# One user per score tile at the end, a shared block of last keys, and a later landing for bulk loads in the planned order

## The chip, the cores and the metric

The kernel runs on one core of a Trainium2 chip, as one program with one launch. The metric is the device time of that program in microseconds; four runs are at hand, and one more execution was profiled. The engines are PE (matrix products; PEld is its loading of weights), DVE, ACT and POOL (elementwise work), and SP, which here only issues DMAs.

## What is computed

Eight batches of eight heads, 576 rows of 64 numbers each. The attention keeps only scores within `tau` = 0.02 of their row's largest, and its output is laid side by side for the eight heads to give 4608 tokens of 512 numbers, which go through a normalised gated feed-forward layer:

```python
scores = scale * np.matmul(q, k.transpose(0, 1, 3, 2))
thresh = np.max(scores, axis=-1, keepdims=True) - tau
scores = np.where(scores >= thresh, scores, -1000000000.0)
scores = scores - np.max(scores, axis=-1, keepdims=True)
attn = np.exp(scores)
attn = attn / (np.sum(attn, axis=-1, keepdims=True) + 1e-09)
x = np.matmul(attn, v)                  # then heads side by side: (4608, 512)
rms = np.sqrt(np.mean(x * x, axis=-1, keepdims=True) + 1e-06)
xn = x / rms * rms_g
g = xn @ w_gate
silu = g * (1.0 / (1.0 + np.exp(-g)))
val = xn @ w_val
out = (silu * val @ w_out)              # (512, 1536), (512, 1536), (1536, 512)
```

## The kernel before

**Tiling.** Every 128 rows of queries make a chunk: four from the first 512 rows of each batch ("m"), and one from the last 64 rows of two batches together ("v"). That gives 36 chunks, and with four pairs of heads each 144 steps. The 576 keys of a head are four blocks of 128 and a last one of 64. For the even head of a pair the probabilities lie as main blocks and then last keys, for the odd head as last keys and then main blocks, so that in the row of 1152 probabilities block 4 of nine holds the last 64 keys of both heads, one above the other.

**A step.** `emit_s` makes the scores on PE (fp32, L566) into the two score tiles `s_ps0` and `s_ps1`, one for each head. Each is 1024 columns of PSUM, two banks; a head's 576 scores lie across the boundary. DVE reads them (`ttr`, L589) and takes the row maxima; POOL makes the threshold (`nth`, L596); ACT, and POOL for some heads, make the probabilities `wsb` in fp16 (L607, L611, L614, L626, L640, L645). They are transposed into `wt`, by PE in the first 16 steps (L659) and by a DMA on SP's queue after that (L674).

**Product with the values.** After every second step `emit_av` multiplies two pairs of heads (L696). For each head it runs five products of 65 columns (64 values and a column of ones that gives the row sum). For the block of last keys it uses entry 8 of `va` for the even head, whose lower 64 rows are zero, and entry 9 for the odd head, whose upper 64 rows are zero. All four heads share one PSUM slot. DVE divides by the row sums (L712, L713) and `emit_x` normalises (L724 to L732) and transposes by DMA (L736).

**Feed-forward.** `emit_ffn` takes groups of two or four chunks (`SIZES`), so products of 256 or 512 columns. For each of twelve blocks of the hidden layer there is a gate product (`gmm`, L790) and a value product (`vmm`, L795), a tanh on ACT (L804), and two steps on DVE: `silu` (L807) and `gate` (L812), whose result is the fp16 block `hf`. The output products follow when all twelve blocks are there, six at a time (L849). Only the last group, of two chunks, is "streamed": its output products (L829) are interleaved with the gate and value products, `OUT_LAG` blocks behind, and two PSUM slots accumulate through the whole group. The result is moved to `osb` by ACT (L863), or for the second chunk of the streamed group by DVE (L861), and stored by SP (L868).

**PSUM slots.** Gate, value and output products, products with the values and transposes share a ring of four slots of one bank, tiles of their own. After the last score step the four banks of the two score tiles become four more slots, 4 and 5 in `s_ps0`, 6 and 7 in `s_ps1` (`opens`, set at L952). PSUM slots are assigned by the plan; waits between instructions are placed by the tile framework from the tiles that they touch.

**The order.** Every piece of work is an `Op` with an engine, an estimated cost, a priority and the pieces that it needs. `order_ops` plays the engines forward in time: it takes, over all engines, the piece that can start first, ties by priority, and writes out that order. Each engine runs its queue in it. A DMA's end is planned from one shared DMA stream (`dma_free`, which advances by the transfer's own `DMA_NS`) plus a latency: `LAT_TR` = 3000 ns for a transposing DMA and 2000 ns for any other. Loads of queries, keys, values and weights that are marked `bulk` may not start more than `BACKLOG` ahead of that stream. At the start the first keys come by ACT's queue (bulk), the first queries and last keys by SP's (`load_q0`, `load_kt`, not bulk).

Of the kernel before, what the change touches and what calls it, by code (L numbers as in the profile page):

```python
# [13 lines left out]
SEM = 160.0  # L14
SLACK = 0.0
COST = dict(
    s_main=932.0, s_virt=900.0, tr_qk=530.0, tr4=230.0, tr_full=440.0, av_main=320.0, av_virt=500.0, ffn4=216.0, warm=3500.0,
    ttr=690.0, evac_qk=600.0, evac_half=380.0, evac_kt=350.0, prelu=700.0, exp2=1250.0, exp1=690.0, exp0=690.0,
    mask_d=750.0, mask_g=1740.0, take_g=1300.0, trw=510.0, evac_w=450.0, evac_wp=900.0, rz=180.0, xmul=420.0, sq=800.0, xn=720.0,
    pool_tiny=270.0, pool_mean=800.0, pool_dma=850.0, cast_v=650.0, cast_vt=420.0, cast_w=720.0,  # L20
# [4 lines left out]


class Op:
    __slots__ = ("eng", "cost", "prio", "deps", "fn", "ring", "frees", "slot", "end", "start", "dma", "opens", "nring", "mode", "bulk", "release")

    def __init__(self, eng, cost, prio, deps, fn, ring=None, frees=None, dma=0.0, nring=1, mode=0, bulk=False):  # L30
        self.eng, self.cost, self.prio, self.fn = eng, cost, prio, fn
        self.deps = [d for d in deps if d is not None]
        self.ring, self.frees, self.dma = ring, frees, dma
        self.slot = self.end = self.start = None
        self.opens = ()
        self.nring = nring
        self.mode = mode
        self.bulk = bulk
        self.release = 0.0


def order_ops(ops, ring_sizes):


    import heapq

    ring_free = {r: [(0.0, i) for i in range(n)] for r, n in ring_sizes.items()}
    users = {}
    left = {}
    for i, o in enumerate(ops):  # L50
        left[i] = len(o.deps)
        for d in o.deps:
            users.setdefault(id(d), []).append(i)
    pending = {}
    for i, o in enumerate(ops):
        pending.setdefault(o.eng, [])
        if not left[i]:
            pending[o.eng].append(i)
    eng_free = {e: 700.0 for e in pending}
    dma_free = 0.0  # L60
    mode = 0
    out = []
    ready_at = {i: 0.0 for i in range(len(ops))}
    while len(out) < len(ops):
        best = None
        for e, lst in pending.items():
            if not lst:
                continue
            t0 = eng_free[e]
            cand = None  # L70
            for i in lst:
                o = ops[i]
                t = max(t0, ready_at[i])
                if o.ring is not None:
                    if len(ring_free[o.ring]) < o.nring:
                        continue
                    t = max(t, sorted(ring_free[o.ring])[o.nring - 1][0])
                other = e == "PE" and o.mode != mode
                t = max(t, o.release)
                if o.bulk:  # L80
                    t = max(t, dma_free - BACKLOG)
                k = (t + (BIAS if other else 0.0), o.prio, i)
                if cand is None or k < cand:
                    cand = k
            if cand is not None and (best is None or cand < best[0]):
                best = (cand, e)
        (t, _, i), e = best
        o = ops[i]
        cost = o.cost
        if e == "PE":  # L90
            if o.mode != mode:
                t -= BIAS
                cost += SWITCH
            mode = o.mode
        o.start = t
        if o.ring is not None:
            o.slot = []
            for _ in range(o.nring):
                got = min(ring_free[o.ring])
                ring_free[o.ring].remove(got)  # L100
                o.slot.append(got[1])
        eng_free[e] = t + cost
        if o.dma:
            dma_free = max(dma_free, t + 300.0) + o.dma
            o.end = max(dma_free, t + o.cost) + (LAT_TR if o.cost == COST["sp_tr"] else 2000.0)
        else:
            o.end = t + cost
        if o.frees is not None:
            ring_free["R"].append((o.end + SEM, o.frees[0].slot[o.frees[1]]))
        for slot in o.opens:  # L110
            ring_free["R"].append((o.end + SEM, slot))
        pending[e].remove(i)
        out.append(o)
        for j in users.get(id(o), []):
            u = ops[j]
            wait = 0.0 if u.eng == o.eng and not o.dma else SEM + (SLACK if u.eng == "PE" else 0.0)
            ready_at[j] = max(ready_at[j], o.end + wait)
            left[j] -= 1
            if not left[j]:
                pending[u.eng].append(j)  # L120
    return out
# [3 lines left out]
def kernel(  # L125
# [12 lines left out]
    nc = tc.nc  # L138
    B, H, S, D = q.shape
# [78 lines left out]
    def add(eng, cost, prio, deps, fn, **kw):  # L218
        o = Op(eng, cost, prio, deps, fn, **kw)
        ops.append(o)  # L220
        return o
# [455 lines left out]
            w_read[s] = t  # L677
            w_ready[s] = [t]

    V_AT = ((0, 2, 4, 6, 8), (9, 1, 3, 5, 7))  # L680

    def emit_av(s):

        ci, p1 = steps[s]
        kind, b, c = chunks[ci]
        hp = p1 // 2

        def fn(o):
            for i in range(2):
                w, p = wt[(s - 1 + i) % NWT], p1 - 1 + i  # L690
                for h in range(2):
                    at = (2 * i + h) * (D + 1)
                    rows = [(slice(0, 128), b % 2)] if kind == "m" else [(HALF[e], e) for e in range(2)]
                    for rs, vi in rows:
                        for j in range(5):
                            nc.tensor.matmul(ring[o.slot[0]][rs, at:at + D + 1], w[:, 4 * h + j, rs],  # L696
                                             va[vi][:, p, V_AT[h][j]], start=(j == 0), stop=(j == 4))

        bs = [b] if kind == "m" else [2 * b, 2 * b + 1]
        deps = w_ready[s - 1] + w_ready[s] + [x for bb in bs for i in range(2) for x in v_ready[bb, p1 - i]]  # L700
        o = add("PE", 2 * COST["av_main" if kind == "m" else "av_virt"], s + AV_PRIO, deps, fn, ring="R",
                mode=0 if kind == "m" else 3)
        for i in range(2):
            av_of[s - i] = [o]
            for bb in bs:
                last_av[bb, p1 - i] = last_av.get((bb, p1 - i), []) + [o]

        r = rz[len(half_ev) % 3]

        def half(_):  # L710
            o3 = ring[o.slot[0]][:, 0:4 * (D + 1)].rearrange("p (h d) -> p h d", d=D + 1)
            nc.vector.reciprocal(out=r, in_=o3[:, :, D])  # L712
            nc.vector.tensor_tensor(  # L713
                out=xsb[ci % 2][:, 256 * hp:256 * hp + 256].rearrange("p (h d) -> p h d", d=D),
                in0=o3[:, :, 0:D], in1=r[:, :, None].to_broadcast([128, 4, D]), op=ALU.mult)

        half_ev.append(add("DVE", COST["rz"] + COST["xmul"], s + HALF_PRIO, [o] + x_done.get(ci - 2, []), half,
                           frees=(o, 0)))
# [48 lines left out]
    def emit_ffn(slot, parts, ready_step, pace, streamed):  # L767
# [55 lines left out]
        if streamed:  # L823

            acc = None
            for fc, (hi, m_) in enumerate(hs):
                def omm(o, fc=fc, hi=hi, first=acc):
                    for j in range(len(parts)):
                        nc.tensor.matmul(ring[(first or o).slot[j]], hf[hi][:, 128 * j:128 * (j + 1)], wo[:, fc],  # L829
                                         start=(fc == 0), stop=(fc == NFC - 1))  # L830

                mo = add("PE", len(parts) * COST["ffn4"], st + dt * (fc + OUT_LAG), [m_] + wo_ld + outs[-1:], omm,
                         ring=None if acc else "R", nring=len(parts))
                acc = acc or mo
                outs.append(mo)
                hf_use[hi] = [mo]
        for j, (ci, _) in enumerate(parts):
# [24 lines left out]
                else:  # L862
                    nc.scalar.activation(out=osb[oi], in_=ring[mo.slot[at]], func=AF.Copy, scale=0.5)  # L863

            def store(o, oi=oi, kind=kind, b=b, c=c):
                if kind == "m":
                    dst = out[b * S:b * S + MAIN].rearrange("(si sc) d -> si sc d", sc=4)[:, c]
                    nc.sync.dma_start(out=dst, in_=osb[oi])  # L868
                else:
                    for e in range(2):  # L870
                        r0 = (2 * b + e) * S + MAIN
# [1 line left out]

            e = add("DVE" if late else "ACT", 690.0 if late else 620.0, pr - PUSH[0], [outs[-1], osb_use.get(oi)], ev,
                    frees=(mo, at))
            osb_use[oi] = add("SP", COST["sp"] if kind == "m" else 1100.0, pr, [e], store, dma=DMA_NS['out'])
        if not streamed:
            for hi, _ in hs:
                hf_use[hi] = list(outs)
# [69 lines left out]
        if step > 0:  # L949
            o.deps.append(s_of[int(step)])  # L950
    for h in range(2):
        ttr_of[len(steps) - 1, h].opens = (4 + 2 * h, 5 + 2 * h)  # L952
    seq = order_ops(ops, {"R": 4})
    global LAST_SEQ
    LAST_SEQ = seq
# [3 lines left out]


PACE = 13.0
NHF = 16
SIZES = (2, 2, 2, 2, 4, 4, 4, 4, 4, 4, 2, 2)
LAG = 16.0
LAT_TR = 3000.0
REL = (0.0, 0.0)
REL_N = (0, 0)
STREAMED = 1
OUT_LAG = 3.0
OUT_PART = 6  # L970
ELAG = 16.0
NELAG = 0
# [58 lines left out]
```

## Time and profile before

| What | Value |
|---|---|
| Median of four runs | 574.64 us (574.57 to 575.74) |
| Profiled execution | 574.66 us, of it the span of the program's instructions 572.9 us |
| Granted TensorE clock | 1.00 |
| DVE, scores to `ssb` (L589) | 288 instructions, mean 753 ns |
| ACT, probabilities (L607) | 224 instructions, mean 766 ns |
| PE, output products in blocks of six (L849), 512 columns | 384 instructions, 89.3 us busy |
| Loads to landing, median | values 3.1 us, keys 3.3, queries 3.2, gate weights 4.2, value weights 4.7 |
| Stores to landing, median | 2.7 us |
| Transposing DMAs of probabilities | 128, 3.1 us to landing |

Times in the views are microseconds from the start of the span unless marked as ns. A line of the timeline gives start, length, engine, line, operation, the tile written and the tiles read, shapes, and how many instructions were merged; in brackets the engine's idle time ahead and what ended it. A line of the chain of waits gives start, length and what was waited for. Matmuls are pipelined and their ends are modelled, so the distance from one start to the next says more of PE than a length.

### The profile page before, as it was taken

How to read it: one execution, taken by the hardware profiler on the slowest of the kernel's cores; microseconds unless marked ns; L12 is line 12 of the kernel's file. 1: busy time of each engine (PE TensorE's matmuls, PEld its weight loads, DVE VectorE, ACT ScalarE, POOL GpSimd, SP SyncE). 2: the span in 40 equal slices, each digit the busy share in tenths (PEclk: the TensorE clock that was granted, in tenths of full speed). 3: DMA queues.
4: the chain of work that ended last, by engine and by line, in shares of the span. 5: the costliest groups of instructions: out<-in, count | busy, mean ns of one | idle time of the engine just before them, and what ended most of it. 6: DMA issues, size and time to landing. Idle time of an engine off the chain costs nothing.

```text
span 572.9 us, 14110 instructions
## 1 busy us (share of the span) xinstructions
PE 560.3 (98%) x5160; PEld 333.9 (58%) x5160; DVE 426.4 (74%) x1093; ACT 459.6 (80%) x739; POOL 322.5 (56%) x462
## 2 busy tenths in 40 slices
PE   8989999999999999999999999999999999999995
PEld 4666776767767555555555455555555455554763
DVE  4898986868958688659974889578867886585543
ACT  3998998998979788879988997888978997883322
POOL 1367856876657456665765667565666665541000
PEclk9999999999999999999999999999999999999999
DMA  7899999768995679968977597867788454641111
GB/s 173 224 268 253 235 178 214 140 134 191 176 195 121 129 156 168 168 172 183 155 181 169 118 167 175 193 165 147 165 193 171 104 105 112 142 93 48 56 38 37
DMA packets 271173, 89.01 MB, mean 155 GB/s; under 512 B 253696, under 2 KB 263424, under 8 KB 271104
## 3 DMA queue, kind: packets, MB, share of 16 engines
q1 hardware_dynamic: 268448, 86.28, 69.4%
q0 software_dynamic: 1600, 1.57, 1.8%
q8 instruction: 40, 0.66, 0.5%
q10 hardware_dynamic: 1056, 0.26, 0.2%
q14 instruction: 29, 0.24, 0.2%
HBM read 37.75 MB, written 9.44 MB: 82 GB/s over the span
## 4 chain that ended last, share of the span: by engine, by line
PE 88%; POOL 3%; DMA 3%; ACT 2%; DVE 2%; issue 2%; SPq 0%; ACTq 0%; DVEq 0%; POOLq 0%
PE s_ps L566 28%; PE ring L795 15%; PE ring L790 15%; PE ring L849 14%; PE ring L696 7%; PE ring L302 2%; DMA vst<-in_v_dram 1%; PE s_ps L790 1%; PE s_ps L795 1%; PE ring L364 1%; PE s_ps L829 1%; PE s_ps L849 1%; ACT ssb L607 1%; DVE ssb L589 1%; DMA qkn<-in_k_dram 1%
## 5 line engine op out<-in xcount | busy, mean ns | idle before, releaser
L589 DVE CUSTOM_DVE_ANT_0 ssb<-s_ps,zrow 128x576 f32<-128x576 f32 x288 | 206.8, 753 | 61.8 <-PE s_ps L566 52.9
L607 ACT ACTIVATE ssb<-ssb,nth 128x576 f32<-128x576 f32 x224 | 165.6, 766 | 26.7 <-POOL nth L596 26.2
L566 PE MATMUL s_ps<-qkt 64*128 64x288 f32 x1024 | 172.3, 432 | 1.4 <-DVE mx L589 1.1
L566 PEld LDWEIGHTS s_ps<-qkt 64*128 64x128 f32 x1024 | 96.4, 187 | 55.7 <-DVE mx L589 14.0
L640 POOL TENSOR_SCALAR wsb<-ssb,nth 128x576 f16<-128x576 f32 x64 | 110.5, 1726 | 11.5 <-ACT ssb L607 3.9
L790 PE MATMUL ring<-xnT,wg 128*128 128x512 f16 (+1 forms) x524 | 108.4, 329 | 0.1
L795 PE MATMUL ring<-xnT,wv 128*128 128x512 f16 (+1 forms) x520 | 107.5, 329 | 0.3 <-DVE xsb L713 0.3
L596 POOL TENSOR_SCALAR nth<-mx 128x2 f32<-128x2 f32 x144 | 31.6, 220 | 133.0 <-DVE mx L589 123.3
L614 ACT ACTIVATE wsb<-ssb 128x1152 f16<-128x1152 f32 x80 | 93.0, 1163 | 2.3
L849 PE MATMUL ring<-wo,hf 128*128 128x512 f16 x384 | 89.3, 380 | 0.0
L804 ACT ACTIVATE th<-ring 128x512 f32<-128x512 f32 (+1 forms) x131 | 63.6, 487 | 29.6 <-PE ring L790 24.1
L645 POOL TENSOR_TENSOR wsb<-wsb,esb 128x576 f16<-128x576 f16 x64 | 81.8, 1278 | 9.7 <-ACT esb L626 4.9
L807 DVE SCALAR_TENSOR_TENSOR sl<-th,ring 128x512 f32<-128x512 f32 (+1 forms) x131 | 72.9, 556 | 15.9 <-ACT th L804 15.5
L812 DVE TENSOR_TENSOR hf<-ring,sl 128x512 f16<-128x512 f32 (+1 forms) x130 | 73.0, 562 | 12.6 <-PE ring L795 4.1
L795 PEld LDWEIGHTS <-wv 128*128 128x128 f16 x576 | 51.7, 98 | 43.9 <-issue 14.5
L790 PEld LDWEIGHTS <-wg 128*128 128x128 f16 x576 | 52.1, 98 | 40.7 <-issue 10.6
L849 PEld LDWEIGHTS <-hf 128*128 128x128 f16 x408 | 37.4, 98 | 47.0 <-issue 6.6
L696 PEld LDWEIGHTS <-wt 128*128 128x128 f16 (+1 forms) x1600 | 51.5, 100 | 18.5 <-issue 9.8
L696 PE MATMUL ring<-va,wt 128*128 128x65 f16 (+1 forms) x1580 | 56.3, 194 | 0.1
L626 ACT ACTIVATE esb<-ssb,nth 128x576 f16<-128x576 f32 x64 | 49.2, 769 | 5.1 <-POOL nth L596 4.9
L611 ACT ACTIVATE wsb<-ssb 128x576 f16<-128x576 f32 x64 | 43.6, 682 | 1.7
L713 DVE TENSOR_TENSOR xsb<-ring,rz 128x256 f32<-128x256 f32 x71 | 30.1, 424 | 2.5
(65 smaller groups left out, 419.9 us busy)
## 6 DMA issues: line engine op xcount, KB each, us to landing
vst<-in_v_dram SPq DMA_DIRECT2D x32, 256.0 KB, 3.1
out_dram<-osb SPq DMA_DIRECT2D x32, 256.0 KB, 2.7
qkn<-in_k_dram SPq DMA_DIRECT2D x62, 128.0 KB, 3.3
qkn<-in_q_dram SPq DMA_DIRECT2D x56, 128.0 KB, 3.2
stage<-in_moe_w_gate_dram SPq DMA_DIRECT2D x12, 256.0 KB, 4.2
stage<-in_moe_w_val_dram SPq DMA_DIRECT2D x12, 256.0 KB, 4.7
wt<-wsb SPq DMA_TRANSPOSE x128, 3.1
wo<-in_moe_w_out_dram POOLq DMA_DIRECT2D x4, 384.0 KB, 6.5
```

The lines of the kernel that those rows point to most:

```text
L566: nc.tensor.matmul(s_ps[h][rows, ROW_AT + n * part:ROW_AT + n * part + n], lhs(hs), kT[i][p][h][hs, n * part:n * part + n], start=True, st ...
L589: nc.vector.tensor_tensor_reduce(out=ssb[a][:, h], in0=s_ps[h][:, ROW_AT:ROW_AT + S], in1=zrow, scale=-1.0 / 8.0, scalar=3.0e38, op0=ALU.a ...
L607: nc.scalar.activation(out=ssb[a][:, h], in_=ssb[a][:, h], func=PRELU, scale=-1.0, bias=nth[m][:, h:h + 1], **PRELU_KW)
L614: nc.scalar.activation(out=wsb[s % NW], in_=ssb[a], func=AF.Exp)
L640: nc.gpsimd.tensor_scalar(out=wsb[s % NW][:, h], in0=ssb[a][:, h], scalar1=nth[m][:, h:h + 1], scalar2=None, op0=ALU.is_le)
L645: nc.gpsimd.tensor_tensor(out=wsb[s % NW][:, h], in0=wsb[s % NW][:, h], in1=esb[es], op=ALU.mult)
L696: nc.tensor.matmul(ring[o.slot[0]][rs, at:at + D + 1], w[:, 4 * h + j, rs], va[vi][:, p, V_AT[h][j]], start=(j == 0), stop=(j == 4))
L790: nc.tensor.matmul(ring[o.slot[0]][:, 0:n], wg[d][:, fs], xnT[slot][:, d, 0:n], start=(d == 0), stop=(d == 3))
L795: nc.tensor.matmul(ring[o.slot[0]][:, 0:n], wv[d][:, fs], xnT[slot][:, d, 0:n], start=(d == 0), stop=(d == 3))
L807: nc.vector.scalar_tensor_tensor(out=sl[i][:, 0:n], in0=th[i][:, 0:n], scalar=1.0, in1=ring[g.slot[0]][:, 0:n], op0=ALU.add, op1=ALU.mult)
L812: nc.vector.tensor_tensor(out=hf[hi][:, 0:n], in0=ring[vv.slot[0]][:, 0:n], in1=sl[i][:, 0:n], op=ALU.mult)
L849: nc.tensor.matmul(ring[(first or o).slot[0]], hf[hs[fc][0]][:, 128 * j:128 * (j + 1)], wo[:, fc], start=(fc == 0), stop=(fc == NFC - 1))
```

## The change

The product with the values takes the block of last keys once for both heads of a pair: one product of 130 columns against entries 8 and 9 of `va` together opens the accumulation, and then each head adds its four main blocks. So a pair has nine products for ten; the planned costs of the two forms are lowered.

At the end only one slot in each score tile is opened, slot 4 in `s_ps0` and slot 6 in `s_ps1`. An `Op` can now name the slots that it may take (`pick`), and the streamed group's accumulators may take only 4 and 6. `OUT_LAG` goes from 3 to 5. The store of the second chunk of the streamed group is issued by ACT in place of SP.

In the plan a bulk load now ends `LAT_LD` = 3000 ns behind its transfer, where it was 2000.

```diff
-    s_main=932.0, s_virt=900.0, tr_qk=530.0, tr4=230.0, tr_full=440.0, av_main=320.0, av_virt=500.0, ffn4=216.0, warm=3500.0,
+    s_main=932.0, s_virt=900.0, tr_qk=530.0, tr4=230.0, tr_full=440.0, av_main=310.0, av_virt=480.0, ffn4=216.0, warm=3500.0,
...
+        self.pick = None
...
                 if o.ring is not None:
-                    if len(ring_free[o.ring]) < o.nring:
+                    free = [f for f in ring_free[o.ring] if o.pick is None or f[1] in o.pick]
+                    if len(free) < o.nring:
                         continue
-                    t = max(t, sorted(ring_free[o.ring])[o.nring - 1][0])
+                    t = max(t, sorted(free)[o.nring - 1][0])
...
-                got = min(ring_free[o.ring])
+                got = min(f for f in ring_free[o.ring] if o.pick is None or f[1] in o.pick)
...
-            o.end = max(dma_free, t + o.cost) + (LAT_TR if o.cost == COST["sp_tr"] else 2000.0)
+            o.end = max(dma_free, t + o.cost) + (LAT_TR if o.cost == COST["sp_tr"] else LAT_LD if o.bulk else 2000.0)
...
-    V_AT = ((0, 2, 4, 6, 8), (9, 1, 3, 5, 7))
...
-                for h in range(2):
-                    at = (2 * i + h) * (D + 1)
-                    rows = [(slice(0, 128), b % 2)] if kind == "m" else [(HALF[e], e) for e in range(2)]
-                    for rs, vi in rows:
-                        for j in range(5):
-                            nc.tensor.matmul(ring[o.slot[0]][rs, at:at + D + 1], w[:, 4 * h + j, rs],
-                                             va[vi][:, p, V_AT[h][j]], start=(j == 0), stop=(j == 4))
+                rows = [(slice(0, 128), b % 2)] if kind == "m" else [(HALF[e], e) for e in range(2)]
+                for rs, vi in rows:
+
+                    at = 2 * i * (D + 1)
+                    nc.tensor.matmul(ring[o.slot[0]][rs, at:at + 2 * (D + 1)], w[:, 4, rs],
+                                     va[vi][:, p, 8:10].rearrange("p e d -> p (e d)"), start=True, stop=False)
+                    for h in range(2):
+                        for j in range(4):
+                            nc.tensor.matmul(ring[o.slot[0]][rs, at:at + D + 1], w[:, 5 * h + j, rs],
+                                             va[vi][:, p, 2 * j + h], start=False, stop=(h == 1 and j == 3))
+                        at += D + 1
...
-                acc = acc or mo
+                if not acc:
+
+                    acc, mo.pick = mo, ACC
...
-                    nc.sync.dma_start(out=dst, in_=osb[oi])
+                    (nc.scalar if late else nc.sync).dma_start(out=dst, in_=osb[oi])
...
-            osb_use[oi] = add("SP", COST["sp"] if kind == "m" else 1100.0, pr, [e], store, dma=DMA_NS['out'])
+            late = late and kind == "m"
+            osb_use[oi] = add("ACT" if late else "SP", COST["sp"] if kind == "m" else 1100.0, pr, [e], store,
+                              dma=DMA_NS['out'])
...
-        ttr_of[len(steps) - 1, h].opens = (4 + 2 * h, 5 + 2 * h)
+        ttr_of[len(steps) - 1, h].opens = OPENS[h]
...
+ACC = (4, 6)
+OPENS = ((4,), (6,))
+LAT_LD = 3000.0
-OUT_LAG = 3.0
+OUT_LAG = 5.0
```

More of the change, by code (lines that the diff above doesn't have):

```diff
@@ L27 @@
 class Op:
-    __slots__ = ("eng", "cost", "prio", "deps", "fn", "ring", "frees", "slot", "end", "start", "dma", "opens", "nring", "mode", "bulk", "release")
+    __slots__ = ("eng", "cost", "prio", "deps", "fn", "ring", "frees", "slot", "end", "start", "dma", "opens", "nring", "mode", "bulk", "release", "pick")
     def __init__(self, eng, cost, prio, deps, fn, ring=None, frees=None, dma=0.0, nring=1, mode=0, bulk=False):
@@ L863, in ev, with store @@
                     nc.scalar.activation(out=osb[oi], in_=ring[mo.slot[at]], func=AF.Copy, scale=0.5)
-            def store(o, oi=oi, kind=kind, b=b, c=c):
+            def store(o, oi=oi, kind=kind, b=b, c=c, late=late):
                 if kind == "m":
                     dst = out[b * S:b * S + MAIN].rearrange("(si sc) d -> si sc d", sc=4)[:, c]
-                    nc.sync.dma_start(out=dst, in_=osb[oi])
+                    (nc.scalar if late else nc.sync).dma_start(out=dst, in_=osb[oi])
                 else:
```

## The prediction

> **What bounds the kernel now.** I read the page's engine line first, then the chain of waits, then the timeline of single stretches: the steady middle, the last 25 us, the first 9 us.
>
> ```profile
> PE 560.3 (98%) x5160; PEld 333.9 (58%) x5160; DVE 426.4 (74%) x1093; ACT 459.6 (80%) x739; POOL 322.5 (56%) x462
> L566 PE MATMUL s_ps<-qkt 64*128 64x288 f32 x1024 | 172.3, 432 | 1.4 <-DVE mx L589 1.1
> L696 PE MATMUL ring<-va,wt 128*128 128x65 f16 (+1 forms) x1580 | 56.3, 194 | 0.1
> ```
>
> PE is the bound, but 98% busy does not say dense: busy time is modelled and overlaps. The start-to-start times say where PE is dense. From the chain of waits (start, length, what, count):
>
> ```profile
> 19.89 1.91 PE s_ps L566 x8
> 22.52 0.50 PE ring L659 x9
> 44.77 6.77 DMA vst<-in_v_dram
> 226.83 1.17 PE s_ps L566 x8
> 512.54 0.61 PE ring L696 x20
> ```
>
> A step's eight score matmuls take 1.17 us all through the middle. 128 such groups would be 149.8 us; they are busy 172.3, so 22.5 us are lost inside them, nearly all in the first 180 us, where lengths of 1.2 to 1.9 us are common and the chain leaves PE (between 30 and 60 us it runs over POOL, SP and DMA). From 180 to 510 us the chain is PE and nothing else: there only fewer PE nanoseconds help. The end shows PE waiting in a pattern (PE rows with ACT and DVE beside them; in brackets the idle time and its releaser):
>
> ```profile
> 549.80 0.60 PE L790 MATMUL s_ps<-xnT,wg 128*128 128x256 f16 x4
> 550.65 0.60 PE L795 MATMUL s_ps<-xnT,wv 128*128 128x256 f16 x4 [0.25 <-ACT osb L863]
> ...
> 552.83 0.60 PE L790 MATMUL s_ps<-xnT,wg 128*128 128x256 f16 x4
> 553.26 0.59 PE L829 MATMUL s_ps<-wo,hf 128*128 128x512 f16 x2
> 553.70 0.60 PE L795 MATMUL s_ps<-xnT,wv 128*128 128x256 f16 x4
> 553.89 0.38 ACT L804 ACTIVATE th<-s_ps 128x256 f32<-128x256 f32 x1 [0.92 <-PE s_ps L829]
> 554.84 0.42 DVE L812 TENSOR_TENSOR hf<-s_ps,sl 128x256 f16<-128x256 f32 x1
> 555.31 0.59 PE L829 MATMUL s_ps<-wo,hf 128*128 128x512 f16 x2 [0.58 <-DVE hf L812]
> ```
>
> The tanh at 553.89 needs only the gate product issued at 552.83, yet it waits for the output product (L829) issued after it in the same tile. The output product at 555.31 is block 1's, whose hidden block was finished at 553.08, yet it waits for a gating (L812) of block 3 that reads the other half of its tile. Two users of one score tile wait for each other though their halves have nothing in common.
>
> **The tail, step by step.** A 256-column product follows the one before after 0.437 us (551.08 to 551.52), a pair of output products too. Read against that, PE loses 550.65 - 549.80 - 0.44 = 0.41 us once; the pattern 554.13 to 555.31 loses 1.18 - 0.44 = 0.74 us, and recurs at 558.79 and 563.45: 3 x 0.74 = 2.22. The group before loses where a third product meets a score tile: 533.89 to 534.62 (0.29), 537.68 to 538.31 and 541.37 to 542.00 (0.19 each). Sum 0.41 + 2.22 + 0.67 = **3.3 us**. With one user per tile (slots 4 and 6 only, and the accumulators picked to lie there) none of these waits is left. The price is eight PSUM slots becoming six, four once the accumulators hold theirs. A gate product's slot is busy from 551.08 to the end of its silu, 552.55: 1.5 us; a value product's from 551.52 to 553.08: 1.6. With outputs interleaved a block takes 3 x 0.437 = 1.31 us of PE and two slots, so four slots come round after 2.62 us. That covers 1.6; if it did not, each block would pay the difference. Next late would be DVE: 0.42 + 0.42 of 1.31 us. The longer lag (5 for 3) only moves output products later; the last six already run without a gap behind the last gating, so I cost it at nothing. If both accumulator slots are rarely free together, output products bunch at the end: the same 24 x 0.2165 us of PE, a cost of 0 to 0.5 us.
>
> **The last store.** It moves from SP's queue to ACT's. Its eviction (L861) starts at 568.30 and takes 0.69, so it ends at 568.99; SP, which issued the other store at 568.70, issues this one only at 569.46:
>
> ```profile
> 568.30 0.69 DVE L861 TENSOR_SCALAR osb<-s_ps 128x512 f32<-128x512 f32 x1 [0.80 <-PE s_ps L829]
> 569.46 0.33 SPq L868 DMA_DIRECT2D out_dram<-osb  x1
> out_dram<-osb SPq DMA_DIRECT2D x1, 256.0 KB, 2.5
> ```
>
> On ACT, whose last work ends at 568.68 and which has nothing queued behind, it can go at about 569.04: **0.4 us** earlier, and it ends the run. Bounds 0 (ACT's issue may take 0.65 us as its two loads at 0.73 do, against SP's 0.33) and 0.47. The Trainium skill, DMA: Bandwidth & Descriptors, "Issuing engines are not separate DMA queues", says that a second issuing engine saves only the sequencer's issue time; by that page the gain is at most SP's 0.33 us, while the row shows a delay of 0.47 behind SP.
>
> **The shared block of last keys.** Per head pair, ten 65-column products become eight and one of 130. In the chain 20 of 65 columns take 0.61 us (30.5 ns each) and nine of 128 columns 0.50 us (55.6 ns). So a product costs about 0.40 ns a column ((55.6 - 30.5) / 63) and 4.6 ns besides; one of 130 columns takes 56.4 ns against 2 x 30.5 = 61. The change spares 1600 - 1440 = 160 products: 160 x 4.6 ns = **0.7 us**. Bounds: 0, and 160 x 30.5 = 4.9 us if the wide one cost no more than a narrow one, which the row of 128 columns makes remote. The spared weight loads hide behind the products (PEld 58%). A rule speaks against this edit: the Trainium skill, TensorE: Matmul & The Clock Gate, "Back-to-back issue gap", gives 81 ns for a 128-column product in a real stream of loads and products. Taking that as an estimate for 130 columns, each pair would lose 81 - 61 = 20 ns and the edit would cost 3.2 us; the row of nine at 55.6 ns says otherwise, and I go by the row.
>
> **The order.** LAT_LD gives each bulk load 3.0 us for 2.0 in the plan. It issues nothing new, but every transpose of queries and keys, every rounding of values and every weight cast is ranked a microsecond later on its in-order queue, and loads that wait for those buffers follow. At the very start I can follow the plan by its own figures. The first keys are due at 0.70 + 0.30 + 1.25 + 3.0 = 5.25 us in place of 4.25. The rest of the first queries is not bulk and stays at 5.15 (its transfer is planned to end at 3.15, plus 2.0). So its transposes now precede the keys' on PE. The trace has both loads:
>
> ```profile
> 5.50 1.08 PE L364 MATMUL ring<-id,qkn 128*128 128x128 f32 x4 [0.69 <-DMA qkn<-in_k_dram]
> 7.02 0.90 PE L364 MATMUL ring<-id,stage 128*128 128x128 f32 x3
> stage<-in_q_dram SPq DMA_DIRECT2D x1, 192.0 KB, 3.8
> ```
>
> Issued at 2.04, the queries land at 5.8, the keys at 5.4. The keys' transposes then start near 6.6 for 5.5, while the queries' and tail keys' copies are out of the way before. I take **+0.3 us** for the first score step, between -0.2 and +0.6. Further on the plan cannot be followed by reading. Gains: waits behind late loads go. POOL's casts stand 4.6 + 2.4 us at loads before 62 us, and PE 1.3 once (38.10, for queries); the chain's DMA pieces there are 3.86 and 6.77 us. Half of 7.0 reaching PE is the gain's end, -3. Losses: the worst disturbance of the old order is at 158 to 164 us, where POOL stands 3.9 us and the value products wait; two score groups after it take 1.91 and 1.54 us for 1.17, the products at 163.45 start late; I price one such at 2.9 us (POOL's 3.9 less the 1 us that slices beside it lose anyway). Nearest is neither end: the stretch after 180 us is dense and forgives reordering. I take 0 for it, -3 to +2.9.
>
> **Sum.** -3.3 - 0.4 - 0.7 + 0.3 + 0 = -4.1 us on a span of 572.9: 568.8. The profiled execution took 574.66, 1.8 us around its span, and the median of the four is 574.64: **570.5 us**.
>
> **Rivals and chances.** A measurement here can tell about 0.2%, 1.15 us, from no change.
> - The sum holds, the order nearly neutral: 570.5, own range 569.0 to 572.0. Chance 0.50.
> - The new order also frees PE in the first 180 us: 570.5 - 3 = 567.5. For it: POOL's 7 us at loads. Against it: PE there is also held by DVE (9.1, 8.9, 9.4 us busy of 10 from 20 to 50 us). Chance 0.19.
> - The new order meets one more pile-up like that at 158 us: 570.5 + 2.9 = 573.4, on the border of no change. Chance 0.15.
> - **Slower**: later ranks bunch the loads of a batch (the six loaded after the first two) ahead of the transposing DMAs of the probabilities on SP's queue; POOL's masks wait for those, scores for the masks. One such place costs 2.9 us as at 158; it decides from two on (4.1 + 1.15 = 5.25 us to lose): 570.5 + 2 x 2.9 = 576.3. For it: POOL's mask once waited 1.7 us for such a DMA (84.88) and once 3.9 us, put down to an ACT instruction that was long done. Against it: in the middle the steps run ahead of PE. Chance 0.11.
> - The change doesn't do what it says: the waits at the end stay, because the accumulators' tiles are still met by others: 574.66 - 0.4 - 0.7 + 0.3 = 573.9. Against it: four ring tiles show no such wait. Chance 0.05.
>
> Faster by over 0.2% (under 573.5): 0.50 + 0.19 + half of 0.15 + 0.01 = 0.77. Within 0.2%: 0.08 + 0.04 = 0.12. Slower: 0.11. The range leaves out the slower case and the far end of the second: 567.0 to 574.3.
>
> **What would show it.** The last group's products at 0.437 us without a gap, and no wait of L829 for L812; a last store from ACT within 0.1 us of its eviction; 18 products of L696 in about 0.60 us where 20 took 0.61; 1280 + 320 such products becoming 1440; the first score step near 8.1 for 7.85 us; score groups in the first 180 us as long as now. The forecast is wrong if a gap reappears once four slots carry the last group, or if the first 180 us shift by more than 3 us.

## The result, and the profile after

The changed kernel takes 572.96 us (median of 50 runs) against 574.84 us for the kernel before (median of 76): the ratio is 0.9962, with a 95% interval of 0.9951 to 0.9974, so by the ratio 2.2 us off (1.5 to 2.8). The forecast was 570.5 us, 4.1 us off, in a range of 567.0 to 574.3. The sign and the range held; a little over half of the gain arrived.

The page of the changed kernel, the lines that answer to those shown of before:

```profile
PE 556.7 (98%) x5000; PEld 334.2 (59%) x5000; DVE 428.2 (75%) x1093; ACT 458.3 (80%) x739; POOL 322.1 (57%) x462
L568 PE MATMUL s_ps<-qkt 64*128 64x288 f32 x1024 | 167.8, 431 | 1.7 <-ACT qkt L376 0.9
L699 PE MATMUL ring<-va,wt 128*128 128x65 f16 (+1 forms) x1264 | 53.4, 194 | 0.0
L695 PE MATMUL ring<-va,wt 128*128 128x130 f16 (+1 forms) x158 | 35.3, 228 | 0.2 <-DMA wt<-wsb 0.2
```

There are 160 matmuls fewer (5160 to 5000). That the two lines of the product with the values are now busy for 53.4 and 35.3 us where one line had 56.3 says nothing yet: busy times of lines overlap, a product is busy for 194 ns while its successor starts 30 ns later. Their cost has to be read from starts.

The last group in the timeline of the changed kernel:

```profile
554.38 0.60 PE L794 MATMUL ring<-xnT,wg 128*128 128x256 f16 x4
554.82 1.03 PE L833 MATMUL s_ps<-wo,hf 128*128 128x512 f16 x4
555.68 0.60 PE L799 MATMUL ring<-xnT,wv 128*128 128x256 f16 x4
556.12 0.60 PE L794 MATMUL ring<-xnT,wg 128*128 128x256 f16 x4
556.55 0.59 PE L833 MATMUL s_ps<-wo,hf 128*128 128x512 f16 x2
556.99 0.60 PE L799 MATMUL ring<-xnT,wv 128*128 128x256 f16 x4
```

Every product starts 0.437 us after the one before (0.87 after the double one), and no bracket is left: the waits of 0.58 us are gone. The end of the run:

```profile
565.00 0.69 DVE L867 TENSOR_SCALAR osb<-s_ps 128x512 f32<-128x512 f32 x1 [1.66 <-PE s_ps L833]
565.41 0.33 SPq L874 DMA_DIRECT2D out_dram<-osb  x1
565.73 0.36 ACTq L874 DMA_DIRECT2D out_dram<-osb  x1
```

The last store goes out at 565.73, 0.04 us after its eviction ends (565.69); before, on SP, 0.47 us passed.

The loss is in the middle, in the eight groups of products of the tail chunks ("v"). First the kernel before, then the changed one, PE's timeline:

```profile
102.76 0.89 PE L696 MATMUL ring<-va,wt 128*64 128x65 f16 x40
103.57 0.61 PE L795 MATMUL ring<-xnT,wv 128*128 128x256 f16 x4
```

```profile
101.32 0.24 PE L695 MATMUL ring<-va,wt 128*64 128x130 f16 x1
101.40 0.32 PE L699 MATMUL ring<-va,wt 128*64 128x65 f16 x5
101.54 0.24 PE L695 MATMUL ring<-va,wt 128*64 128x130 f16 x1
101.56 0.38 PE L699 MATMUL ring<-va,wt 128*64 128x65 f16 x8
101.75 0.24 PE L695 MATMUL ring<-va,wt 128*64 128x130 f16 x1
101.77 0.38 PE L699 MATMUL ring<-va,wt 128*64 128x65 f16 x8
101.96 0.24 PE L695 MATMUL ring<-va,wt 128*64 128x130 f16 x1
101.99 0.47 PE L699 MATMUL ring<-va,wt 128*64 128x65 f16 x11
102.39 0.51 PE L568 MATMUL s_ps<-qkt 64*128 64x288 f32 x2
```

Before, 40 products took 0.82 us from their start to the next group's (102.76 to 103.57). Now 36 take 1.07 (101.32 to 102.39): 20 ns a product became 30. In a tail chunk each product fills 64 of the array's 128 columns (the 128*64 in the lines), for one of two batches. Before, five of one half were followed by five of the other; now nine by nine. All eight such groups show the same two lengths, 0.81 to 0.82 and 1.06 to 1.07 us.

### The profile page after: what moved, and what is told of

Same layout as the page of the kernel before. It is cut to its first block, busy times and chain, and to the rows that moved or that the text cites. A ratio compares the mean times of both kernels' runs of the same rounds, so it can differ in the third digit from the quotient of the medians.

```text
span 569.4 us, 13799 instructions
## 1 busy us (share of the span) xinstructions
PE 556.7 (98%) x5000; PEld 334.2 (59%) x5000; DVE 428.2 (75%) x1093; ACT 458.3 (80%) x739; POOL 322.1 (57%) x462
## 4 chain that ended last, share of the span: by engine, by line
PE 89%; DMA 5%; DVE 3%; POOL 1%; issue 1%; SPq 1%; ACT 0%; DVEq 0%; POOLq 0%
PE s_ps L568 28%; PE ring L794 16%; PE ring L799 15%; PE ring L855 15%; PE ring L699 6%; DMA qkn<-in_q_dram 2%; PE ring L695 2%; PE ring L304 2%; DVE ssb L591 1%; PE s_ps L794 1%; PE s_ps L833 1%; PE s_ps L855 1%; DMA wt<-wsb 1%; PE s_ps L799 1%; PE ring L366 1%
## 5 line engine op out<-in xcount | busy, mean ns | idle before, releaser
L568 PE MATMUL s_ps<-qkt 64*128 64x288 f32 x1024 | 167.8, 431 | 1.7 <-ACT qkt L376 0.9
L568 PEld LDWEIGHTS s_ps<-qkt 64*128 64x128 f32 x1024 | 94.8, 187 | 53.1 <-DVE mx L591 14.3
L799 PE MATMUL ring<-xnT,wv 128*128 128x512 f16 (+1 forms) x544 | 111.7, 328 | 0.9 <-DVE xsb L717 0.6
L794 PE MATMUL ring<-xnT,wg 128*128 128x256 f16 (+1 forms) x540 | 110.9, 328 | 0.5 <-DVE xsb L717 0.3
L811 DVE SCALAR_TENSOR_TENSOR sl<-th,ring 128x512 f32<-128x512 f32 (+1 forms) x135 | 74.6, 553 | 29.6 <-ACT th L808 28.8
L808 ACT ACTIVATE th<-ring 128x512 f32<-128x512 f32 (+1 forms) x135 | 65.3, 485 | 30.4 <-PE ring L794 27.5
L816 DVE TENSOR_TENSOR hf<-ring,sl 128x512 f16<-128x512 f32 (+1 forms) x136 | 76.1, 560 | 10.7 <-PE ring L799 0.8
L699 PE MATMUL ring<-va,wt 128*128 128x65 f16 (+1 forms) x1264 | 53.4, 194 | 0.0
L699 PEld LDWEIGHTS <-wt 128*128 128x128 f16 (+1 forms) x1280 | 49.2, 100 | 3.6
L695 PE MATMUL ring<-va,wt 128*128 128x130 f16 (+1 forms) x158 | 35.3, 228 | 0.2 <-DMA wt<-wsb 0.2
```

The costliest lines, as they stand in the source:

```text
L568: nc.tensor.matmul(s_ps[h][rows, ROW_AT + n * part:ROW_AT + n * part + n], lhs(hs), kT[i][p][h][hs, n * part:n * part + n], start=True, st ...
L699: nc.tensor.matmul(ring[o.slot[0]][rs, at:at + D + 1], w[:, 5 * h + j, rs], va[vi][:, p, 2 * j + h], start=False, stop=(h == 1 and j == 3))
L794: nc.tensor.matmul(ring[o.slot[0]][:, 0:n], wg[d][:, fs], xnT[slot][:, d, 0:n], start=(d == 0), stop=(d == 3))
L799: nc.tensor.matmul(ring[o.slot[0]][:, 0:n], wv[d][:, fs], xnT[slot][:, d, 0:n], start=(d == 0), stop=(d == 3))
L811: nc.vector.scalar_tensor_tensor(out=sl[i][:, 0:n], in0=th[i][:, 0:n], scalar=1.0, in1=ring[g.slot[0]][:, 0:n], op0=ALU.add, op1=ALU.mult)
L816: nc.vector.tensor_tensor(out=hf[hi][:, 0:n], in0=ring[vv.slot[0]][:, 0:n], in1=sl[i][:, 0:n], op=ALU.mult)
```

## The experiments

All ratios are to the kernel before, run on the same chip beside them. Runs of one kernel spread over some 5 us on one chip (573.7 to 578.6 in 25 runs of the kernel before), so a ratio's interval is as important as the ratio, and small terms are read in the profiles.

**The end alone.** The kernel before with the edits to its end and nothing else (fewer slots opened, `pick`, the longer lag, the last store from ACT; the main lines stand below); until the last score step every queue keeps its order.

```diff
-        ttr_of[len(steps) - 1, h].opens = (4 + 2 * h, 5 + 2 * h)
+        ttr_of[len(steps) - 1, h].opens = OPENS[h]
...
+                    acc, mo.pick = mo, ACC
...
-                    nc.sync.dma_start(out=dst, in_=osb[oi])
+                    (nc.scalar if late else nc.sync).dma_start(out=dst, in_=osb[oi])
...
-OUT_LAG = 3.0
+OUT_LAG = 5.0
```

> The kernel before with only the end of the change (one slot in each score tile, accumulators on slots 4 and 6, lag 5, last store from ACT). Every queue's order is that of before until the last score step. Theory: the false waits are the whole loss of the end, so 3.3 + 0.4 us come off: 571.1 against 574.8, and the last group's products follow each other after 0.437 us. Rival: the end gave less and the order took nothing back, so the whole change's 1.9 us are the end's: 572.9.

Measured: 571.77 us, ratio 0.9924 (0.9896 to 0.9953), so 4.4 us off (2.7 to 6.0). Sharper is the profile, since the work behind the last score step is the same in both. From the start of the last score group to the end of the last output product, first before, then the end alone:

```profile
508.60 1.24 PE L566 MATMUL s_ps<-qkt 64*128 64x288 f32 x8
...
566.80 1.46 PE L829 MATMUL s_ps<-wo,hf 128*128 128x512 f16 x6
```

```profile
507.67 1.24 PE L568 MATMUL s_ps<-qkt 64*128 64x288 f32 x8
...
561.68 2.32 PE L831 MATMUL s_ps<-wo,hf 128*128 128x512 f16 x10
```

568.26 - 508.60 = 59.66 us before, 564.00 - 507.67 = 56.33 now: 3.3 us, the sum of the prediction to the tenth. The rival, that the end gave no more than the whole change, falls.

**The shared block alone.** The kernel before with the new `emit_av` and its old planned costs, so that the order stays.

```diff
-    V_AT = ((0, 2, 4, 6, 8), (9, 1, 3, 5, 7))
...
+                    nc.tensor.matmul(ring[o.slot[0]][rs, at:at + 2 * (D + 1)], w[:, 4, rs],
+                                     va[vi][:, p, 8:10].rearrange("p e d -> p (e d)"), start=True, stop=False)
```

> The kernel before with only the shared block of last keys; planned costs as before, so every queue's order stays. Theory, from the two traces: a product with the values of a full chunk takes 0.65 us in both forms, of a chunk of tails 0.82 us before and 1.07 after, eight times, so +2.0 us: 576.8. Rival (the prediction's term): 160 products fewer spare 0.7 us, 574.1.

Measured: 576.83 us, ratio 1.0012 (0.9992 to 1.0032), 0.7 us more (-0.5 to 1.8). Neither figure fits: -0.7 lies just below the interval, +2.0 just above it. The profile has both parts: groups of a full chunk last 0.61 us in the median for 0.62 before, so 64 x 12 ns = 0.8 us gained, and the eight groups of tail chunks 1.07 for 0.82, so 2.0 lost. The sum, +1.2, lies inside; I had left the gain out.

**The later landing alone.** The kernel before with one planned latency changed; the same instructions in another order on every queue.

```diff
-            o.end = max(dma_free, t + o.cost) + (LAT_TR if o.cost == COST["sp_tr"] else 2000.0)
+            o.end = max(dma_free, t + o.cost) + (LAT_TR if o.cost == COST["sp_tr"] else LAT_LD if o.bulk else 2000.0)
```

> The kernel before with only the later landing of bulk loads in the plan; same instructions in another order. Theory: the order is close to neutral, within 1 us of 574.8 (the end and the values' product explain -3.7 + 2.0 = -1.7 of the measured -1.9). Rival: the new order costs about 2 us, 576.8, and takes back what the end gave.

Measured: 577.54 us, ratio 1.0037 (1.0014 to 1.0059), 2.1 us more (0.8 to 3.4). In this plan the rival holds: the edit alone makes the kernel slower. In the profile of before no wait of PE of 0.2 us or more stands between 62 and 550 us; here six do, 3.6 us in all. The longest is for a load of queries, the next on DVE's queue (PE and DVE rows of the timeline):

```profile
99.25 0.46 PE L304 MATMUL ring<-id,qkn 64*128 64x64 f32 x8 [1.26 <-DMA qkn<-in_q_dram]
...
276.90 0.76 DVE L591 CUSTOM_DVE_ANT_0 ssb<-s_ps,zrow 128x576 f32<-128x576 f32 x1 [0.51 <-PE s_ps L568]
277.70 0.43 DVE L452 COPY qkt<-ring 64x256 f32<-64x256 f32 x1
278.16 0.76 DVE L591 CUSTOM_DVE_ANT_0 ssb<-s_ps,zrow 128x576 f32<-128x576 f32 x1
278.18 1.02 PE L797 MATMUL ring<-xnT,wv 128*128 128x512 f16 x4 [0.93 <-DVE qkt L452]
```

The value product needs the slot that the copy of the last keys holds, and that copy now stands behind one more reading of scores (276.90). How much of the six waits reaches the end wasn't settled: profiles of other kernels with the order of before show one to five such waits too, and the score groups got shorter in turn (below, under the order).

**The changed kernel without the later landing.** Whether that price belongs to the edit or to one plan:

```diff
-LAT_LD = 3000.0
+LAT_LD = 2000.0
```

> The changed kernel with bulk loads landing 2.0 us after their transfer in the plan, as before. If the later landing costs 2 us in this plan as it does alone, this is 2 us faster than the changed kernel, ratio 0.9925. If the cost of the later landing belongs to the one plan that it was tried in, and any other reshuffle may go either way, it lies within 1 us of the changed kernel, 0.9945 to 0.998.

Measured: 573.30 us, ratio 0.9964 (0.9947 to 0.9981), the changed kernel's 0.9962 again. With the planned costs of the shared block, which reshuffle the order too, the landing shows no price either way, to about 1.2 us.

**The changed plan with the old product.** The changed kernel with `emit_av` of before and the new planned costs, so with the changed order throughout.

> The changed kernel with the product with the values as it was (ten products for each pair of heads), the changed plan kept, so every queue's order is that of the changed kernel. It splits the loss: theory, the form of the tail chunks' product alone costs 8 x 0.25 = 2.0 us of the changed kernel, so 571.0 on the first scale (a ratio to before near 0.993) and the changed order costs nothing worth naming beside the end's gain. Rival: the changed order costs the 2 us that the later landing costs alone, and the product little; then the ratio stays at 0.996.

Measured: 571.21 us, ratio 0.9926 (0.9906 to 0.9946), against 0.9962 for the changed kernel: the form of the product costs it 0.36%, 2.1 us (0.8 to 3.4 from the two intervals). The edit swaps the whole product, for which the profiles give 1.2 us, 2.0 lost less 0.8 gained; that lies inside too. The changed order shows no price beside the end alone (0.9924), but these two intervals leave it some 2 us either way. The rival, a ratio of 0.996, falls.

**The halves in turn.** The changed kernel, where in a tail chunk the two halves' products alternate; the same instructions, nothing else moves.

```diff
-                for rs, vi in rows:
-                    at = 2 * i * (D + 1)
-                    nc.tensor.matmul(ring[o.slot[0]][rs, at:at + 2 * (D + 1)], w[:, 4, rs],
...
-                    for h in range(2):
-                        for j in range(4):
-                            nc.tensor.matmul(ring[o.slot[0]][rs, at:at + D + 1], w[:, 5 * h + j, rs],
+                at = 2 * i * (D + 1)
+                for rs, vi in rows:
+                    nc.tensor.matmul(ring[o.slot[0]][rs, at:at + 2 * (D + 1)], w[:, 4, rs],
...
+                for h in range(2):
+                    for j in range(4):
+                        for rs, vi in rows:
+                            nc.tensor.matmul(ring[o.slot[0]][rs, at:at + D + 1], w[:, 5 * h + j, rs],
```

> The changed kernel, but in a chunk of tails the products of the two 64-column halves take turns instead of running nine of one half and then nine of the other; nothing else moves. Theory: the halves run side by side in the array only where they are near each other in the queue, so 36 products take about 18 x 31 ns = 0.56 us for 1.07, eight times: 4 us less than the changed kernel, 569.0. Rival: the wide product or something else makes the tail chunks slow, and the time stays at 573.

Measured: 571.59 us, ratio 0.9917 (0.9888 to 0.9945), 0.45% under the changed kernel, 2.6 us. The profile, the same group:

```profile
103.10 0.25 PE L694 MATMUL ring<-va,wt 128*64 128x130 f16 x2
103.18 0.42 PE L699 MATMUL ring<-va,wt 128*64 128x65 f16 x16
103.43 0.23 PE L694 MATMUL ring<-va,wt 128*64 128x130 f16 x2
103.49 0.42 PE L699 MATMUL ring<-va,wt 128*64 128x65 f16 x16
103.84 0.51 PE L568 MATMUL s_ps<-qkt 64*128 64x288 f32 x1
```

0.74 us for 1.07, eight times: 2.6 us, as measured. Products of the two halves now start in pairs 3 to 4 ns apart, a pair every 31 ns. My 0.56 us forgot that two pairs are of 130 columns (0.08 and 0.06 us to the next pair) and that 0.12 us pass from the last pair to the next group.

**The halves in turn, ten products.** The kernel before with the two inner loops exchanged, to see the turn without the wide product.

```diff
-                    for rs, vi in rows:
-                        for j in range(5):
+                    for j in range(5):
+                        for rs, vi in rows:
```

> The kernel before with the ten products of each head of a tail chunk issued in turn for the two halves in place of five and five. One look at the profile, where a group of 40 is read directly. Theory (halves run beside each other only where they are near each other in the queue, and five and five is near enough): the group stays at 0.82 us or falls a little. Rival (only strict turns run side by side fully): it falls to 0.62, 40 x 31 / 2.

One profiled execution:

```profile
103.83 0.82 PE L696 MATMUL ring<-va,wt 128*64 128x65 f16 x40
104.59 0.61 PE L795 MATMUL ring<-xnT,wv 128*128 128x256 f16 x4
```

The group of 40 lasts 0.76 us (103.83 to 104.59): a little less, as the theory said. Of both lengths 0.13 us pass between the last product and the next group; without them turns take 0.63 us, near the rival's 0.62, and five and five 0.69. So turns are the best, and five and five is near them. The length follows how many products of one half stand in a row: 0.74 to 0.76 us for one, 0.82 for five, 1.07 for nine. The wide product is not to blame: it is there in the 0.74 too.

**Both banks open.** The changed kernel with slots 4 to 7 opened at the end, the accumulators on 4 and 6 as before.

```diff
-OPENS = ((4,), (6,))
+OPENS = ((4, 5), (6, 7))
```

> The changed kernel with both banks of each score tile opened as slots at the end (4 to 7), the accumulators still on 4 and 6; nothing moves ahead of the last score step. One look, read in the profile of the last 25 us. Theory (two users of one tile wait for each other though their banks differ): gate or value products that land on 5 and 7 bring back waits of L833 for L816 of about 0.7 us each, so PE from the last score step to its end takes 1 to 3 us more than in the changed kernel. Rival (the accumulators' place or the lag did it): no such waits, the same length.

One profiled execution, the timeline's last group:

```profile
555.32 0.42 DVE L816 TENSOR_TENSOR hf<-s_ps,sl 128x256 f16<-128x256 f32 x1
555.37 0.38 ACT L808 ACTIVATE th<-ring 128x256 f32<-128x256 f32 x1 [0.70 <-PE ring L794]
555.79 0.42 DVE L811 SCALAR_TENSOR_TENSOR sl<-th,ring 128x256 f32<-128x256 f32 x1
555.80 0.38 PE L833 MATMUL s_ps<-wo,hf 128*128 128x512 f16 x1 [0.15 <-DVE hf L816]
```

The accumulating product waits again for the gating that reads the other bank of its tile and ends at 555.74. From the last score group to the end of the last output product it takes 62.27 us (504.23 to 566.50) for 59.76 in the changed kernel (505.20 to 564.96): 2.5 of the 3.3 us are back. (That the 59.76 is no less than the 59.66 of before is the changed order: it leaves 16 more products of 512 columns, 16 x 0.2165 = 3.5 us, behind the last score group.) The waits have other sizes than the expected 0.7 us: the longest bracket is 0.73, for an eviction, the others 0.15 to 0.30. With the lag and the accumulators' place kept, opening the second banks brought most of the loss back, so it was mainly one user in each tile that had removed it. The remaining 0.8 us wasn't taken apart.

**Lag three.** The changed kernel with `OUT_LAG` back at 3.

> The changed kernel with output products three blocks behind in place of five; nothing moves ahead of the end. One look. Theory (costed at nothing): PE from the last score step to its end keeps its length within 0.3 us, all products at 0.437 us. Rival (the longer lag is needed to get both accumulator slots, or hides the last gating): gaps of 0.3 us or more in the last group.

One profiled execution: 506.58 to 566.35, 59.77 us, without a gap. The lag does nothing, as it was costed.

**What the runs pointed to.** The order of before, the changed end, and the shared block with the halves in turn.

> The order of before (planned costs and landing as before), the changed end, and the shared block of last keys with the two halves of a tail chunk in turn. Theory: the end's -4.4, nothing for the order, and 8 x (0.74 - 0.82) = -0.6 for the product: ratio 0.991, below the changed kernel's 0.996 and near the end alone. Rival: the terms don't add, because time freed ahead of the last score step is lost again at the loads; then no faster than the end alone, 0.9924.

Measured: 569.85 us, ratio 0.9909 (0.9879 to 0.9939), 5.2 us off (3.5 to 7.0). It is the lowest of all, below the changed kernel (the intervals don't meet); from the end alone and from the changed kernel with the halves in turn it can't be told apart.

## Why the prediction was right, and where it was not

- **The bound.** PE, dense in the middle: held. A quarter or a third of a microsecond in each of eight PE groups arrived at the end of the run, added or taken away, within the intervals.
- **The tail, -3.3.** Held to the tenth in the profile of the end alone, and 2.5 of it undone with both banks open. Four slots carried the last group, as 1.6 of 2.62 us had said.
- **The last store, -0.4.** The head start came, the gain only in part. SP issued it 0.47 to 0.49 us after the eviction in four profiles, ACT 0.03 in eight. But from issue to landing SP's took 2.5 to 2.6 us and ACT's 2.5 to 3.2. From the eviction's end to landing SP needed 2.96 to 3.04 us, in the mean 3.0. ACT needed 2.49 to 2.78 in the six profiles with a changed order, in the mean 2.7, and 3.22 and 3.24 in the two with the order of before. So the term was worth 0.3 us in the changed kernel and was lost in the other two; why the landing differs wasn't tried. The prediction took the whole head start for gain.
- **The shared block, -0.7.** This is the step that failed. For the 64 groups of full chunks, with 128 of the products, the term was about right: 0.6 us by 4.6 ns each, 0.8 measured, and products of 130 columns cost 57 to 58 ns in the median where 56.4 was worked out. But the prediction multiplied by all 160 spared products, and took the price of a product from full chunks, where they follow one another. In tail chunks they run side by side, which the trace of before already showed in the 20 ns of a product there (0.82 / 40) against 30.5. The edit also moved the loop over halves outward, so nine products of one half stand in a row, and the overlap shrank: +2.0 us, undone by taking turns (-2.6, past the old state). The prediction's lower bound for this term was 0; that the edit could cost time by its loop order stood in no term and no rival.
- **The rule weighed there.** The Trainium skill, TensorE: Matmul & The Clock Gate, "Back-to-back issue gap", would have charged the width; the 57 to 58 ns say again that the width is not the price. The same page has the mechanism that mattered in "Part 3: Packing small matmuls — row/col tiling": products in different parts of the array run at the same time, started about 4 ns apart. The trace agrees with 3 to 4 ns.
- **The start, +0.3.** The order at the start came as worked out: queries ahead of keys. The first reading of scores lies at 8.2 to 10.1 us in six profiles with the old start and at 8.8 to 10.0 in six with the new, in the mean 8.9 and 9.4; it can't be told from the spread.
- **The order, 0 between -3 and +2.9.** Held for the changed plan, by 0.9926 against 0.9924, as far as these intervals go. That it was a draw and no property of the edit shows in the later landing alone, which cost 2.1 us. Nor is the zero an order that does nothing: the score groups of full chunks (L566, now L568) are busy for 167.5 to 169.2 us in the six profiles with the later landing and for 171.3 to 172.5 in the six without, though the prediction had expected them as long as now. What takes these 2 to 5 us back wasn't traced; new waits of PE, for queries and for DVE, are a part.

With the sizes as measured the sum closes: -3.3 - 0.3 - 0.8 + 2.0 = -2.4 us, and -2.2 was measured (1.5 to 2.8 off). So for the start and the order together 0.2 us is left, give or take 0.7.

That the result lay in the range was in part luck: the range was wide for the order's sake, and the loss came from the product. The middle case's own range, 569.0 to 572.0, was missed by up to 1 us. The rival nearest to the result, 573.4, stood for a pile-up in the order, and the profile of the changed kernel has none: no wait of PE over 0.63 us between 62 and 550 us.

## What to carry to other kernels

Price an instruction in each place where it runs: products that use half the array overlapped here only with near neighbours in the queue, so a loop moved outward cost more than the instructions that it saved, and taking turns cost nothing. When two users of one buffer have nothing in common and still wait for each other, look at what the waits are tracked by; here half the buffers, each with one user, beat all of them. A change to a planner's figure is a new draw for the whole order: measure it by itself and with the other edits, since its worth in one plan says little of the next.

## What the runs showed of the hardware that I had not expected

In these traces products of the second half of the array overtake those of the first in the queue. In the changed kernel a tail group is issued as one wide and eight narrow products of the first half, and then the second half's wide one. The trace has that wide product at 101.54 us, when only five of the eight narrow ones have started: a look-ahead of about three. In the kernel before, where five stand in a row, the second half's first product starts at 102.81, when two of the five have started: three ahead again. That fits that runs of five lost little and runs of nine much; no run changed the look-ahead itself.

The same instructions in the same order begin at two paces. Before and the end alone, PE's timeline:

```profile
5.50 1.08 PE L364 MATMUL ring<-id,qkn 128*128 128x128 f32 x4 [0.69 <-DMA qkn<-in_k_dram]
7.85 2.10 PE L566 MATMUL s_ps<-qkt 64*128 64x288 f32 x8
```

```profile
4.82 1.09 PE L366 MATMUL ring<-id,qkn 128*128 128x128 f32 x4
6.95 1.43 PE L568 MATMUL s_ps<-qkt 64*128 64x288 f32 x8
```

The first keys landed later in one, and the first score group took 2.10 us for 1.43; why, wasn't tried. So the first scores are read at 10.0 and at 8.2 us, and at step 16 the two are still 1.6 us apart (57.0 and 55.4). That can be part of the spread of some 5 us between runs of one kernel, and is more than several terms of this sum.
